# A state-space scan and an expert layer in one program: the opening's gates and logarithms taken from TensorE to VectorE and through DRAM

## The chip, the cores and the metric

The program runs on one core of one Trainium2 chip. The time is the device time of one execution in microseconds (us). Before the change it is 612.76 us, the median of 3 runs (612.08 to 614.41). One more execution was taken with the hardware profiler; it took 615.48 us, of which the span from the first to the last instruction is 613.8 us.

Engines are named as in the profile: PE is TensorE (PEld its weight loads), DVE is VectorE, ACT is ScalarE, POOL is GpSimd, SP is SyncE, which only issues DMAs here.

## The reference, cut to what matters

All numbers are float32. The first half is a chunked scan over 4 batches x 8 heads x 768 positions, the second half a layer of 4 experts on the 3072 tokens that come out of it.

```python
# per batch and head; chunks of 32 positions
log_a = log(clip(a, 1e-6, 1));  cum = cumsum(log_a in the chunk)
M     = (C @ B.T) * exp(cum[i] - cum[j]) * (i >= j)
y     = M @ x + (C @ state) * exp(cum)[:, None]
state = exp(cum[-1]) * state + sum_j exp(cum[-1] - cum[j]) * outer(B[j], x[j])
# tokens: y of all heads side by side, (3072, 256)
p   = domain_probs / (domain_probs.sum(-1) + 1e-9)
out = sum over experts e of  p[:, e] * (relu(y @ w1[e]) @ w2[e])
```

## The kernel before

The scan is worked off in 12 steps p of 64 positions (p = 2k + e: k is a chunk of 128 positions of each sequence, e its half), four sequences at a time. Each step needs: `scores` (C times B, L499), a decay matrix MT, `masked` (scores times MT, L675), `inner` products with x (L532), the product of C with the carried state (`cts` times S, L911, in `outputs`), and `state` (L541). For p under 3 the matrix MT comes from a running product on DVE (`scan`, L507) over rows of a that PE has spread over the partitions (`spread`, L652); from p = 3 on it is exponents on ACT (`decay`, L515) of sums of logarithms that come back from DRAM (`cum_d` as tiles `ab`) with a negated copy `neg` as bias. The carried state is faded by `dec`, the exponents of `ah`, which is read from another layout of the same sums in DRAM (`cumh_d`).

The expert layer multiplies with fewer products by sums of blocks: operand sums are made by POOL and DVE (`difference`, L1038), products are all one helper, L978 (`product`), results are gated (`gated`, L1013: Relu and gate in one DVE instruction, gate tiles read from `p_d` in DRAM), accumulated through ACT copies (L987, L992, L1278), and combined at the end (L1314). The last block's result is turned by PE (L1384), copied (L1397) and stored (L1389) piece by piece: piece 0 by two DMAs of POOL, the others by SP and ACT.

The order of the opening (L560 to L777) is written by hand: loads, clip of a, the scans of step 0, its scores, masks, inner products and state, and in between the work that prepares steps 1 and 2 and the later sums. In this part PE

- turns the gates `pc` (four transposes, L634), which ACT copies to `p_sb` (L636), and spreads the first gate over all partitions (`spread_gate`, L641, copied at L645); `p_sb` is stored to `p_d` late (L770);
- turns the logarithms (`turn_logs`, L688, copied at L689), sums them by products with a triangle `upto` (`sum_logs`, L693, copied at L696, stored at L699, L702 and L705), and makes the negated sums (`minus_logs`, L712, copied at L718);
- spreads the rows of part 1 of a (`spread(a_q, 1, ...)`) and of the next a (`a_q2`) before, between and behind the inner products.

Everything after that is given to a planner (`Plan`): each piece of work has engines that may do it, a cost, what it reads and writes, and a due time; PE's order is the given `line`, and the other engines' orders follow from a simulation of times that begins at constants (`now`, `START`, begin times for each engine). `OWN`, `SCORED`, `FILLED` and such say how many products stand ahead of which step and how banks of PSUM are handed out. Each engine then runs its own list strictly in order, and a DMA on SP, ACT or POOL stands in that engine's list as well. Eight semaphores serve SP's and ACT's DMAs in turn, so a DMA also waits until the one eight places ahead of it has landed.

The first products are four `plain_first` (two products each, on w1 blocks 0 to 3 and the first tokens yT0), then `scores(1)`, then `own_[:OWN]` products with w2, then `outputs(1)`.

Of the kernel before, what the change touches and what calls it, by code (L numbers as in the profile page):

```python
# [10 lines left out]
ALU = mybir.AluOpType  # L11
# [24 lines left out]
SCORED, OWN, LEAD, LEFT = 7, 4, 5, 4  # L36
FILLED, EARLY = 2, 4
# [33 lines left out]
class Plan:  # L71
# [109 lines left out]
    def run(self, line, at, begin):  # L181
# [17 lines left out]
        self.stall, self.port, self.bus = [], 0.0, begin["SP"] + 3  # L199
        self.lanes = [begin["SP"] + .5 * i for i in range(LANES)]  # L200
# [159 lines left out]
def kernel(  # L360
# [38 lines left out]
    p_d = tc.dram_tile([E * NC, 2, NSEQ, HALF], FP32, name="p_d")  # L399
    w_d = {}  # L400
# [8 lines left out]
    def some(n, shape, name, pool=const):  # L409
# [21 lines left out]
        "dram": [None, None],  # L431
# [26 lines left out]
    def load_carried(p, ah):  # L458
        k, e = divmod(p, 2)
        src = cumh_d.rearrange("(z k q) t e i -> k e z (q t) i", k=NC, q=NQ)[k, e]  # L460
        for z in range(NSEQ):
            nc.sync.dma_start(out=ah[:, z], in_=src[z].unsqueeze(1).to_broadcast([NH, N, HALF]))
# [11 lines left out]
    def load_w2(fb, w):  # L474
        e, f = divmod(fb, EPB)
        nc.sync.dma_start(
            out=w.rearrange("p (j m) -> p j m", j=JJ),
            in_=w2[e, f * FB:f * FB + FB].rearrange("(j p) m -> p j m", p=P))
# [84 lines left out]
    pc = const.tile([P, NSEQ, E, NC], FP32)  # L563
# [10 lines left out]

    for s, queue in enumerate((nc.sync, nc.scalar)):
        load_a(0, s, a_q, queue)
        load_heads(0, bct[0], slice(2 * s, 2 * s + 2), queue)
    nc.scalar.preload_act_table_set("natural_log_exp_and_others")
    for c in range(2):
        load_tokens(0, c, xt[0][:])  # L580
    nc.sync.dma_start(
        out=a_sb, in_=a.rearrange("c h s -> (c h) s").rearrange("(p r) s -> p r s", r=2))
    tmask = const.tile([P, NT], FP32)
    nc.vector.memset(tmask, 0.0)
    nc.vector.memset(a_q2, 0.0)
    for s in range(2):
        load_a(1, s, a_q2, nc.sync)
    for fb in range(4):
        load_w1(fb, homes["W"][fb])
    for fb in range(2):  # L590
        load_w2(fb, homes["W"][4 + fb])
# [18 lines left out]
    def ready(v, e):  # L610
# [11 lines left out]
    upto = const.tile([P, P], FP32)  # L622
    nc.gpsimd.memset(upto, 1.0)
    nc.gpsimd.affine_select(
        out=upto, in_=upto, compare_op=ALU.is_ge, fill=0.0, base=0, pattern=[[1, P]],
        channel_multiplier=-1)
    nc.gpsimd.memset(upto[:HALF, HALF:], 0.0)
    BANK = homes["bank"]
    rows = E * NC
    p_sb = homes["V"][0][:rows].rearrange("p e (z i) -> p e z i", z=NSEQ)  # L630

    def turn_gates(bank):
        for z in range(NSEQ):
            nc.tensor.transpose(  # L634
                bank[:rows, z * P:z * P + P], pc[:, z].rearrange("p e k -> p (e k)"), ident)
        nc.scalar.copy(  # L636
            out=p_sb.rearrange("p e z i -> p z e i"),
            in_=bank[:rows].rearrange("p (z e i) -> p z e i", z=NSEQ, e=2))

    def spread_gate(bank, gate):  # L640
        nc.tensor.matmul(  # L641
            out=bank[:, :FB], lhsT=ident[:rows, 0:1].to_broadcast([rows, P]),
            rhs=p_sb[:, 0].rearrange("p z i -> p (z i)"), start=True, stop=True,
            skip_group_check=True)
        nc.scalar.copy(  # L645
            out=gate[:, :2].rearrange("p c x -> p (c x)"), in_=bank[:, :FB])
# [36 lines left out]
    n = NSEQ * NC * NQ  # L683
    turned = homes["W"][-3][:, :2 * n].rearrange("p (t i) -> p t i", t=NT)

    def turn_logs(bank):
        for t in range(NT):
            nc.tensor.transpose(bank[:, FB + t * n:FB + t * n + n], a_sb[:, t], ident[:n, :n])  # L688
        nc.scalar.copy(out=turned, in_=bank[:, FB:FB + 2 * n].rearrange("p (t i) -> p t i", t=NT))  # L689

    def sum_logs(bank):
        for t in range(NT):
            nc.tensor.matmul(  # L693
                out=bank[:n, FB + t * P:FB + t * P + P], lhsT=turned[:, t], rhs=upto,
                start=True, stop=True, skip_group_check=True)
        nc.scalar.copy(  # L696
            out=homes["cum"][1].rearrange("p e (t i) -> p t e i", t=NT),
            in_=bank[:n, FB:].rearrange("p (t e i) -> p t e i", t=NT, e=2))
        nc.scalar.dma_start(  # L699
            out=cumh_d.rearrange("a t e i -> a e t i")[:, 1],  # L700
            in_=homes["cum"][1][:, 1].rearrange("p (t i) -> p t i", t=NT))
        nc.sync.dma_start(  # L702
            out=cum_d.rearrange("a e t i -> a (e t i)"),
            in_=homes["cum"][1].rearrange("p e x -> p (e x)"))
        nc.sync.dma_start(  # L705
            out=cumh_d.rearrange("a t e i -> a e t i")[:, 0],
            in_=homes["cum"][1][:, 0].rearrange("p (t i) -> p t i", t=NT))

    def minus_logs(bank):
        for s in range(2):  # L710
            for e in range(2):
                nc.tensor.matmul(  # L712
                    out=bank[HALF * s:HALF * s + HALF, FB + e * n:FB + e * n + n].rearrange(
                        "p (t i) -> p t i", t=NT),
                    lhsT=upto[:, HALF * e:HALF * e + HALF],
# [962 lines left out]
```

## Time and profile before

| what | value |
|---|---|
| median of 3 runs | 612.76 us (612.08 to 614.41) |
| profiled execution | 615.48 us, span 613.8 us, granted TensorE clock 0.997 |
| PE busy | 602.8 us, 98% of the span |
| DVE, ACT, POOL busy | 492.8, 276.3, 134.2 us |
| HBM | 72.79 MB read, 20.17 MB written |
| first product of the expert layer | 14.23 us after the span's start |
| last store issued | 609.19 us, end of the span 613.8 us |

How to read it: the busy share of PE says that the time is PE's work plus the few places where PE has none. Those places are the opening (before 14.23), single waits, and the end. The page's sections give shares over the whole span; a table by stage, the timeline and the chain of waits give the places. Times in the timeline and in the chain are us from the span's start. "issue" as a releaser means that the engine waited for nothing that the profile shows. A DMA's line shows the time that its issue took in the queue of the issuing engine, not the transfer.

### The profile page before, as it was taken

What the parts mean: (1) busy time and instruction counts of PE and PEld (TensorE: products, weight loads), DVE (VectorE), ACT (ScalarE), POOL (GpSimd) and SP (SyncE); (2) the same over time, 40 slices, a digit from 0 to 9 for tenths busy, and PEclk for the clock granted to TensorE, in tenths of its full rate; (3) what the DMA queues carried; (4) which work ended last, traced back from release to release, by engine and by line L of the source; (5) the groups of instructions that cost most, each with busy time, mean ns of one, the idle gap of its engine ahead of it and who ended that gap; (6) DMA issues with size and microseconds to landing.
All of it is one profiled execution on the core that took longest, in us unless ns stands there. A gap on an engine that the chain in (4) does not pass through costs nothing.

```text
span 613.8 us, 12211 instructions
## 1 busy us (share of the span) xinstructions
PE 602.8 (98%) x4528; PEld 517.5 (84%) x4528; DVE 492.8 (80%) x858; ACT 276.3 (45%) x623; POOL 134.2 (22%) x143
## 2 busy tenths in 40 slices
PE   9989999999999999999999999999999999999996
PEld 5768888888888888888888888878888888888886
DVE  5659999999999985687988988386785989575794
ACT  3338547675442626764343343434444242434440
POOL 4743554746500100358401000000000000000000
PEclk9989999999999999999999999999999999999999
DMA  6686578879723329763422425953241322954002
GB/s 179 169 250 208 170 191 257 252 230 285 254 77 115 89 33 336 223 224 131 144 82 72 125 34 161 303 170 114 69 133 67 110 72 45 362 190 131 1 0 53
DMA packets 98801, 93.78 MB, mean 153 GB/s; under 512 B 33405, under 2 KB 67933, under 8 KB 98741
## 3 DMA queue, kind: packets, MB, share of 16 engines
q1 hardware_dynamic: 97704, 92.10, 49.2%
q8 instruction: 36, 0.59, 0.4%
q10 hardware_dynamic: 940, 0.63, 0.4%
q0 software_dynamic: 96, 0.26, 0.2%
q14 instruction: 25, 0.20, 0.1%
HBM read 72.79 MB, written 20.17 MB: 151 GB/s over the span
## 4 chain that ended last, share of the span: by engine, by line
PE 89%; DVE 5%; issue 1%; DMA 1%; POOL 1%; ACT 1%; SPq 1%; POOLq 0%; DVEq 0%
PE bank L978 84%; PE bank L532 2%; DVE v L1013 1%; DVE v L1005 1%; PE bank L911 1%; DVE bank L1136 1%; PE bank L499 1%; PE bank L541 1%; POOL w L1038 1%; DMA gate<-p_d 1%; PE bank L652 0%; DMA xt<-in_xbc_dram 0%; DVE MT L520 0%; DVE MT L507 0%; DMA pr<-in_probs_dram 0%
## 5 line engine op out<-in xcount | busy, mean ns | idle before, releaser
L978 PE MATMUL bank<-v,w 128*128 128x256 f32 x1876 | 436.7, 381 | 4.1 <-issue 3.0
L978 PEld LDWEIGHTS bank<-v,w 128*128 128x128 f32 x1876 | 356.0, 191 | 55.5 <-issue 4.2
L978 PE MATMUL bank<-Y,w 128*128 128x256 f32 x692 | 177.2, 381 | 0.3 <-DVE bank L1136 0.3
L1005 DVE TENSOR_TENSOR v<-v,v 128x512 f32<-128x512 f32 x241 | 174.4, 744 | 1.8
L1278 ACT COPY v<-bank 128x512 f32<-128x512 f32 x120 | 70.4, 587 | 202.3 <-PE bank L978 198.3
L978 PEld LDWEIGHTS bank<-Y,w 128*128 128x128 f32 x692 | 130.5, 190 | 19.9 <-ACT v L987 0.9
L1013 DVE SCALAR_TENSOR_TENSOR v<-bank,gate 128x512 f32<-128x512 f32 x162 | 110.9, 686 | 43.5 <-PE bank L978 39.5
L1038 POOL TENSOR_TENSOR w<-w,w 128x512 f32<-128x512 f32 (+1 forms) x82 | 91.1, 1122 | 99.8 <-DMA xt<-in_xbc_dram 35.9
L992 ACT COPY bank<-v 128x512 f32<-128x512 f32 x141 | 81.6, 593 | 19.1 <-DVE v L1013 16.9
L987 ACT COPY v<-bank 128x512 f32<-128x512 f32 x111 | 65.2, 588 | 52.8 <-PE bank L978 45.9
L1136 DVE TENSOR_TENSOR bank<-bank,v 128x512 f32<-128x512 f32 x92 | 62.5, 693 | 32.4 <-PE bank L978 21.1
L1389 POOL DMA_DIRECT2D out_dram<-v x2 | 1.4, 713 | 261.6 <-DVE v L1397 261.6
L515 ACT ACTIVATE MT<-ab,neg 128x64 f32<-128x64 f32 x144 | 37.4, 339 | 0.0
L1005 DVE TENSOR_TENSOR v<-bank,v 128x512 f32<-128x512 f32 x30 | 20.6, 687 | 10.2 <-PE bank L978 7.4
L873 POOL TENSOR_TENSOR cts<-ctm,dec 128x512 f32<-128x512 f32 x11 | 14.9, 1356 | 47.4 <-DVE F L524 31.4
L1314 DVE TENSOR_TENSOR v<-v,v 128x256 f32<-128x256 f32 x64 | 24.2, 415 | 1.0 <-ACT v L1278 0.7
L1013 DVE SCALAR_TENSOR_TENSOR v<-v,gate 128x512 f32<-128x512 f32 x30 | 24.0, 798 | 0.5
L930 ACT COPY v<-bank 64x256 f32<-64x256 f32 (+1 forms) x33 | 12.3, 373 | 18.5 <-PE bank L541 15.4
L675 DVE TENSOR_TENSOR MT<-bank,MT 128x256 f32<-128x256 f32 x47 | 16.7, 412 | 0.7 <-PE bank L499 0.7
L520 DVE TENSOR_TENSOR MT<-MT,bound 128x512 f32<-128x512 f32 x18 | 15.6, 878 | 0.0
L489 ACT ACTIVATE ctm<-bct,tmask 128x256 f32<-128x256 f32 (+1 forms) x26 | 11.2, 485 | 9.4 <-POOL w L1038 5.1
L1005 POOL TENSOR_TENSOR v<-v,v 128x512 f32<-128x512 f32 x9 | 11.5, 1272 | 16.8 <-DVE v L1005 9.1
(96 smaller groups left out, 192.1 us busy)
## 6 DMA issues: line engine op xcount, KB each, us to landing
w<-w_d SPq DMA_DIRECT2D x128, 256.0 KB
w<-in_w_dram SPq DMA_DIRECT2D x72, 256.0 KB
w_d<-w SPq DMA_DIRECT2D x64, 256.0 KB
gate<-p_d SPq DMA_DIRECT2D x15, 384.0 KB
xt<-in_xbc_dram SPq DMA_DIRECT2D x48, 96.0 KB
ab<-cum_d SPq DMA_DIRECT2D x36, 128.0 KB
bct<-in_xbc_dram SPq DMA_DIRECT2D x5, 512.0 KB
out_dram<-v SPq DMA_DIRECT2D x144, 16.0 KB
```

The source lines that it names most:

```text
L515: nc.scalar.activation(out=MT[:, q, c, t], in_=ab[:, c, h], func=AF.Exp, bias=neg[:, e, t, i:i + 1])
L520: nc.vector.tensor_tensor(out=v, in0=v, in1=bound.unsqueeze(1).to_broadcast([P, 4 * n, HALF]), op=ALU.min)
L675: nc.vector.tensor_mul(v, bank[:, FB * half:FB * half + FB], v)
L978: nc.tensor.matmul(out=o, lhsT=w[:, j], rhs=x if half is None else x[:, j], start=(start and j == 0), stop=(j == 1), skip_group_check=True)
L987: act(.5, lambda e: nc.scalar.copy(out=flat(v), in_=bank.t), reads=[bank], writes=[v])
L992: act(.54 if to - lo > FB else .32, lambda e: nc.scalar.copy(out=bank.t[:, lo:to], in_=flat(v)[:, lo:to]), reads=[v], writes=[bank])
L1005: plan.add(engines, lambda e: (on(e).tensor_add if sign > 0 else on(e).tensor_sub)(flat(v), whole(x), whole(y)), reads=[x, y], writes=[v], ...
L1013: dve(D512, lambda e: nc.vector.scalar_tensor_tensor(out=h.t, in0=whole(x).rearrange("p (j m) -> p j m", j=JJ), scalar=0.0, in1=g.t[:, 2 * ...
L1038: (on(e).tensor_add if sign > 0 else on(e).tensor_sub)(out, x, y)
L1136: dve(D512, lambda e: (nc.vector.tensor_add if sign > 0 else nc.vector.tensor_sub)(to.t, bank.t, whole(x)), reads=[x, bank], writes=[to])
L1278: act(.5, lambda e: nc.scalar.copy(out=flat(v), in_=bank.t), reads=[bank], writes=[v], hold=HOLD)
L1314: plan.add(engines, lambda e: (on(e).tensor_add if sign > 0 else on(e).tensor_sub)(o[1](), x[1](), y[1]()), reads=[v for v in vs if v is n ...
```

## The change

In words: the gates `pc` are laid out in four padded groups of 32 columns, turned in 32 x 32 blocks by one DVE instruction, stored to `p_d` by four DMAs (two of SP, two of POOL), and the first gate tile is read back, spread over the partitions, by a DMA of SP. The logarithms are taken with a layout that puts each part's 64 positions side by side, and are summed by one DVE scan with a reset at each start; ACT's and SP's stores follow. The negated sums are made later, in the plan: a DVE turn, three stores to a new DRAM tensor `cumt_d`, two loads, and one ACT instruction (`minus_sums`; its DMAs stand on SP). All six late spreads stand ahead of the inner products; clip and memset of `a_q2` stand ahead of the first scans, and `a_q2` is loaded by ACT. Both halves of `bct` are loaded by SP. Three of the first four w1 blocks are loaded behind the gates' first two stores, the first two w2 blocks by POOL, one half of step 1's tokens (`xt[1]`) earlier, `ah` of step 1 by ACT. The first four gated results are made by Relu on ACT and a product on DVE (or POOL) instead of one DVE instruction. `upto` is gone; `bound` is made by itself. The last stores of piece 0 go by SP and ACT. Constants of the planner are changed; `OWN` goes from 4 to 5.

Program lists of the two kernels differ on PE in the opening (13 products and transposes fewer, one idle product more) and in the place of one product; from there on PE's order is the same. The lists of DVE, ACT, POOL and SP are ordered anew by the planner.

```diff
-SCORED, OWN, LEAD, LEFT = 7, 4, 5, 4
-FILLED, EARLY = 2, 4
+SCORED, OWN, LEAD, LEFT = 7, 5, 5, 4
+FILLED, EARLY = 3, 4
...
-    pc = const.tile([P, NSEQ, E, NC], FP32)
+    pc, turned = (homes["V"][0][:, i, :P] for i in range(2))
+    rows = E * NC
...
+    def store_gates(x, queue):
+        e, h = divmod(x, 2)
+        queue.dma_start(
+            out=p_d[:, e, :, 32 * h:32 * h + 32],
+            in_=turned[32 * x:32 * x + rows].rearrange("r (z i) -> r z i", z=NSEQ))
+
     for s, queue in enumerate((nc.sync, nc.scalar)):
         load_a(0, s, a_q, queue)
-        load_heads(0, bct[0], slice(2 * s, 2 * s + 2), queue)
+    for s in range(2):
+        load_heads(0, bct[0], slice(2 * s, 2 * s + 2))
     nc.scalar.preload_act_table_set("natural_log_exp_and_others")
+    tmask = const.tile([P, NT], FP32)
+    nc.vector.memset(tmask, 0.0)
+    nc.vector.memset(a_q2, 0.0)
+    for s in range(2):
+        load_a(1, s, a_q2, nc.scalar)
...
-    for s in range(2):
-        load_a(1, s, a_q2, nc.sync)
-    for fb in range(4):
-        load_w1(fb, homes["W"][fb])
-    for fb in range(2):
-        load_w2(fb, homes["W"][4 + fb])
+    load_w1(0, homes["W"][0])
...
+    def take_logs():
+        nc.scalar.activation(
+            out=logs.rearrange("p e (t i) -> p t e i", t=NT),
+            in_=a_sb.rearrange("p t (e i) -> p t e i", e=2), func=AF.Ln)
+
+    def sum_logs():
+        nc.vector.tensor_tensor_scan(
+            out=cum.rearrange("p e x -> p (e x)"), data0=reset[:ROWS].rearrange("p x i -> p (x i)"),
+            data1=logs.rearrange("p e x -> p (e x)"),
+            initial=0.0, op0=ALU.mult, op1=ALU.add)
+        for e, queue in ((1, nc.scalar), (0, nc.sync)):
+            queue.dma_start(
+                out=cumh_d.rearrange("a t e i -> a e t i")[:, e],
+                in_=cum[:, e].rearrange("p (t i) -> p t i", t=NT))
         nc.sync.dma_start(
+            out=cum_d.rearrange("a e t i -> a (e t i)"), in_=cum.rearrange("p e x -> p (e x)"))
+        load_tokens(1, 1, xt[1][:])
...
+    nc.vector.transpose(turned, pc)
+    for x in range(4):
+        store_gates(x, nc.gpsimd if x > 1 else nc.sync)
+    for fb in range(1, 4):
+        load_w1(fb, homes["W"][fb])
+    load_tokens(1, 0, xt[1][:])
+    nc.sync.dma_start(
+        out=homes["gate"][0][:, :2].rearrange("p c s -> p (c s)"),
+        in_=p_d[:1, 0].rearrange("x z i -> x (z i)").partition_broadcast(P))
+    ready(a_q2, 0)
...
-    turn_gates(four[2])
-    for s in range(2):
-        score(0, ctm[0], bct[0], seven, 0, s)
-    aside(2, seven[2])
-    spread(a_q, 1, four, 1, (3, 0))
+    score(0, ctm[0], bct[0], seven, 0, 0)
+    spread(a_q, 1, four, 1, ORDER[:2])
+    idle(four[2], 0, 1)
+    score(0, ctm[0], bct[0], seven, 0, 1)
+    spread(a_q, 1, four, 1, ORDER[2:])
+    spread(a_q2, 0, four, 0, ORDER)
...
+    fade_first(0)
+    aside(2, seven[2])
+    fade_first(1)
...
-    spread(a_q, 1, four, 1, (1, 2))
...
-    ready(a_q2, 0)
-    turn_logs(As[1])
     state(F[0], xt[0], As, 0, True)
-    spread(a_q2, 0, four, 0, ORDER)
-    sum_logs(As[0])
-    nc.sync.dma_start(out=p_d, in_=p_sb)
-    for c in range(2):
-        load_tokens(1, c, xt[1][:])
     keep_state(homes["A"][0], As, 0)
-    minus_logs(ys[0])
+    sum_logs()
+    for fb in range(2):
+        load_w2(fb, homes["W"][4 + fb], nc.gpsimd)
...
-    now, START = 9.4, 11.3
+    now, START = 9.7, 10.3
...
+        by, queue = ("SP", nc.sync) if p > 1 else ("ACT", nc.scalar)
+        plan.add({by: ISSUE * 4}, lambda e: load_carried(p, s["ah"].t, queue), lag=LANDING + 256 / 190, kb=256,
+                 pieces=4, part=[s["ah"]], reads=[cd])
...
+    def gated_aside(x, g, n):
+        h = value("V")
+        act(.5, lambda e: nc.scalar.activation(out=flat(h), in_=x.t, func=AF.Relu), reads=[x], writes=[h])
+        plan.add(B512, lambda e: on(e).tensor_mul(
+            h.t, h.t, g.t[:, 2 * n:2 * n + 2].rearrange("p c s -> p (c s)").unsqueeze(1).to_broadcast(
+                [P, JJ, FB])), reads=[g], writes=[h], two=True)
+        return h
...
-        return seq, gated(b, gate_of(0, fb), 0)
+        return seq, gated_aside(b, gate_of(0, fb), 0)
...
-            by = ((nc.sync, "SP"), (nc.scalar, "ACT")) if n else ((nc.gpsimd, "POOL"),) * 2
+            by = ((nc.sync, "SP"), (nc.scalar, "ACT"))
...
+    def minus_sums():
+        v, d = value("V"), value("dram")
+        dve(.4, lambda e: nc.vector.transpose(v.t[:ROWS, 0], sums.t.rearrange("p e x -> p (e x)")),
+            reads=[sums], writes=[v])
...
+        act(.35, lambda e: nc.scalar.mul(neg.t, neg.t, -1.0), writes=[neg])
```

## The prediction

> **What bounds the kernel now.** I read the page's busy times first, then its clock and queue rows, then a table by stage, the timeline of PE around its one hole, and the chain of waits in the opening.
>
> The page; then the table by stage (stretch, its length, busy us and instructions by engine, granted clock, DMA share, GB/s):
>
> ```profile
> PE 602.8 (98%) x4528; PEld 517.5 (84%) x4528; DVE 492.8 (80%) x858; ACT 276.3 (45%) x623; POOL 134.2 (22%) x143
> ...
> PEclk9989999999999999999999999999999999999999
> ...
> q8 instruction: 36, 0.59, 0.4%
> ```
>
> ```profile
> 9.40:14.23 4.83, 4.65 (x136) 3.15 (x135) 2.24 (x7) 1.85 (x5) 2.74 (x7) 1.00 0.82 252
> 14.23:25.96 11.73, 11.45 (x82) 9.40 (x80) 9.83 (x20) 2.44 (x8) 9.17 (x12) 1.00 0.56 165
> 25.96:37.10 11.14, 11.14 (x317) 8.71 (x318) 5.52 (x15) 6.21 (x17) 7.19 (x8) 1.00 0.79 227
> 37.10:40.11 3.01, 0.00 (x1) 0.00 (x0) 3.01 (x6) 0.31 (x2) 1.98 (x3) 1.00 0.79 270
> 40.11:44.20 4.09, 4.09 (x12) 3.30 (x12) 1.85 (x4) 0.37 (x1) 0.56 (x1) 0.58 0.72 220
> 44.20:100.00 55.80, 55.45 (x549) 46.24 (x548) 52.97 (x88) 34.68 (x99) 25.71 (x23) 1.00 0.66 196
> 100.00:600.00 500.00, 499.01 (x3317) 434.87 (x3316) 406.72 (x688) 225.78 (x483) 80.82 (x70) 1.00 0.48 146
> ```
>
> PE is the bound: from 44.2 to 600 it is idle for 1.3 us. The change touches none of those products (FILLED, for the planner's banks, moves by one), so it can act in four places: before the first product at 14.23, in the wait at 25.96, in the hole at 37.10 with the slow clock behind it (0.58), and behind the last product. The timeline shows the wait and the hole, the chain what the opening's end is made of (start, length, what):
>
> ```profile
> 25.96 0.67 PE L911 MATMUL bank<-cts,S 32*32 32x128 f32 x32 [0.29 <-POOL cts L873]
> ...
> 40.11 4.22 PE L978 MATMUL bank<-v,w 128*128 128x256 f32 x11 [3.01 <-issue]
> ```
>
> ```profile
> 5.44 1.86 DVE MT L507 x3
> ...
> 9.47 1.35 PE bank L532 x64
> 10.82 0.59 PE bank L652 x8
> 11.41 0.33 PE bank L688 x2
> ...
> 12.13 0.45 PE bank L541 x30
> 12.59 0.62 PE bank L652 x16
> 13.20 0.62 PE bank L693 x4
> 13.82 0.02 issue
> ```
>
> **The opening.** From the first scan (5.44) to the first product (14.23) the old path is 2.43 (four scans) + 1.53 (second scores, masks; until 9.40) + 1.42 (inner products) + 0.59 (spreads) + 0.33 (logarithms turned) + 0.39 (ACT's copy of them) + 0.45 (state) + 0.62 (spreads) + 0.62 (sums) + 0.41 (negated sums) = 8.79. Turn, copy, sums and negated sums go: 1.75. The gates' turn (0.60) and spread (0.69) lay in PE's waits; they give nothing. The six late spreads move ahead of the inner products. There the last two of part 1 (0.30) and a_q2's four (0.65) stand behind the last scan, because they overwrite banks that scans read; they cover the masks (0.42) and most of the old 1.53, whose other cause, the second half of bct (masked until 7.70), is issued earlier, by SP at once behind the first. New path: 2.43 + 0.95 + 1.42 + 0.55 (state; yT's copies, 0.42, lie beside it) = 5.35, so 3.44 less.
>
> Against it: a_q2's clip (0.42) and memset (0.06) now stand ahead of the scans on DVE. All four scans are queued behind them, and PE, POOL's ends and ACT's aside wait for the scans. a_q2 moves from SP to ACT, behind the table load (1.28 us in the trace). If ACT's queue issues it beside that load, from 2.8 on in 2 x 0.58, and it lands 1.0 later (ACT's first half of a: issue ended at 2.75, DVE's clip began at 3.76), it is there at 5.0, and with the gates' turn and the clip the scans start at 5.7. If it is issued behind the load, it is there at 6.3 and the scans start at 6.8; with the 1.5 that SP's a_q2 took to land, 7.3. I take 6.3, the middle, 0.86 late. VectorE's turn of the gates (128x128; the 128x512 form takes 0.69, so 0.2 to 0.4) fits ahead of it. Opening: 3.44 - 0.86 = **2.6**, first product at 11.65 (11.0 to 12.7).
>
> Who comes too late then? The first w1 no longer waits behind a_q2 on SP and lands before its old 9.8; the other three, behind two gate stores (0.56 each), are due 1.7 us apart: hidden. The first gate goes SP store at about 6.7, load at 10.4, landed near 13; DVE asks for it after the sum scan (0.6) and four scans, at 14.7: hidden by 1.7, beyond that each us holds three scans, F, S and the masks on DVE. SP waits at the sums' stores with xt's second half, two w2 and bct behind it, as it did until 14.24. POOL issues two gate stores ahead of its end copies (0.82 and 0.60 in the last rows) and two w2: 2.9 us; the w2 are due 7.8 us after the first product. ACT issues four loads of ah (2.5) with three of four new Relu copies (0.59 each) behind them: the carried chain ends some 9 us after the first product, PE asks at 12.5, against 11.7 before, so the 0.29 goes: **-0.3**. The negated sums go through DRAM with 5 DMAs behind eight of ab; ACT wants them at 50.7 (first exponents): hidden by several us, else ACT's snaps wait and PE with them. DVE's total hardly moves: four gate products from SBUF (0.74 for 0.69), one scan, two transposes, two F fewer. Reordering by new planner constants may open waits of the kind seen (0.2 to 0.7 each): 0 to 2, **+0.6**.
>
> **The hole.** "issue" means that no semaphore held PE, in the middle of a product. q8 carried 36 packets of 16 KB of instructions (0.59 MB), and PE has 2 x 4,528: 252 for each packet. So I read q8 as PE's instruction feed, and the hole as PE having run out. The trace's packets on q8 start at 12.2, 15.8, 28.2, then 37.55, inside the hole, after SP had issued some 2.5 MB from 25 to 32; PE resumed at 40.11. The change takes 20 matmuls and 20 loads from PE ahead of it (4 + 2 + 2 + 4 + 8) and adds 2 + 2: 36 instructions fewer, so PE reaches 18 products further on what it holds, 18 x 0.224 = 4.0 us, past the 3.01. If the packet comes when the DMA backlog clears, the hole goes, and with it the slow clock, 4.09 x (1 - 0.58) = 1.7: **-4.7**. If it comes a fixed time after PE's place, about 2.6 later here, 1.6 us stay. Worst, it is as long: 0. I take -4.7, since SP's loads of that stretch are spread wider (one waits for a gate buffer, bct behind a POOL sum).
>
> [...]
>
> **The end.** POOL's stores of the first piece (0.82, 0.60 from 608.11) go to SP and ACT, about 0.5 each; ACT's stands ahead of a copy of 0.27. The last stores, issued at 609.19, are not moved: -0.7 to +0.3, **-0.2**.
>
> **Sum.** -2.6 - 0.3 - 4.7 - 0.2 + 0.6 = -7.2: the profiled execution's 615.48 (span 613.8 and 1.7 around it) becomes 608.3. It stands 2.7 above the median 612.76. If that is constant, 605.6; if timed runs have a shorter hole, the hole can give only 2.0 there, and 608.3 stays. Nothing separates these; I take the middle, **607.0**, own range 604.5 to 609.
>
> **Rivals.** *The hole stays* (moved by 18 products): 612.76 - 2.6 - 0.3 - 0.2 + 0.6 = 610.3, to 611.5 with more waits. For it: the packet may be late because PE's sequencer asks late, at a place in the code; then the 36 instructions shift the hole and its length stays, and one late packet can't tell. Against: the other packets came in time with DMA less loaded, and 4.0 is more than 3.01. 0.2.
>
> *The clock falls in the opening.* Between 6.4 and 9.7 PE now waits scan by scan, about half idle; a granted 0.58 over the inner and first products costs 1.7 as after the hole, and a_q2 late 1.0 more: 608.7 to 609.7. Against: 4.29 to 9.40 ran at 1.00 with PE busy for 4.83 of 5.11, and an idle matmul is put in. 0.12. [...]
>
> *The gates come late, and it is slower.* The nearest round trip through DRAM, the sums' (stored 14.24, dec at 22.48), took 8.2; from 6.7 that is 14.9, where DVE asks. DVE's list from the first gate product to the last mask is 7.3 us in the trace's rows, to 22.0; PE asks for the masks at 24.1, so 2.1 are free, and past 17 each us costs PE one. Slower by over 0.5% needs all gains and 3.1 more eaten: landing past 25. Against: only two small stores and one load. 0.07.
>
> Nothing comes of the opening and the hole is absent in timed runs: about 612.5, 0.06.
>
> **Chances.** Forecast 0.55. 0.5%, about what can be told from no change here, is 3.1 us: faster means below 609.7: the forecast, a third of the first rival, most of the second: 0.67. Within: 0.24; slower: 0.09. Range 604.5 to 611.5: forecast's low end, first rival's high end.
>
> **What would show it.** First L965 product at 11.0 to 12.7, the first scan near 6.3; no "issue" of over 1 us on PE, and a 9 in the third place of PEclk, now 8; outputs at L898 waiting for nothing; PE idle under 3 us from 44 to 600. Wrong: a hole with a clock near 0.58 anywhere, or DVE L1011 ended by a DMA of gate.

## The result and the profile after

The changed kernel takes 611.81 us in the median of 20 runs (609.60 to 614.07), the kernel before, on the same chip, 613.85 (20 runs, 612.08 to 616.05). The ratio is 0.9962 with a 95% interval of 0.9948 to 0.9975: faster by 0.4%, where 0.9% was forecast (607.0 from 612.76). That is within the 0.5% that the prediction counted as no change, and 0.3 us outside its range. The profiled execution took 612.63 us, its span is 610.91 (before 613.77).

The page of the changed kernel:

```profile
PE 601.5 (98%) x4510; PEld 516.8 (85%) x4510; DVE 494.8 (81%) x855; ACT 277.9 (45%) x623; POOL 143.8 (24%) x152
...
PEclk7999999999999999999999999999999999999999
...
q8 instruction: 35, 0.57, 0.4%
```

The low digit of the clock has moved from the third place to the first. The table by stage (columns as in the prediction):

```profile
8.46:14.97 6.51, 6.38 (x141) 4.87 (x139) 2.39 (x7) 1.24 (x4) 4.68 (x11) 0.50 0.82 257
14.97:27.33 12.36, 12.36 (x84) 10.29 (x84) 11.42 (x22) 4.33 (x11) 6.25 (x9) 0.99 0.55 154
27.33:39.18 11.85, 11.00 (x317) 8.27 (x316) 8.24 (x17) 6.60 (x19) 7.55 (x9) 1.00 0.67 205
44.20:100.00 55.80, 54.80 (x547) 45.87 (x546) 53.44 (x88) 35.89 (x105) 30.93 (x27) 1.00 0.78 225
100.00:600.00 500.00, 498.75 (x3317) 434.96 (x3316) 405.31 (x680) 223.75 (x475) 87.70 (x77) 1.00 0.47 145
```

In the last 6.5 us of the opening the granted clock is 0.50, and there is no stretch with PE at 0.00 any more. PE's idle time from 44 to 100 is 1.0 us; it was 0.35. PE's timeline where the wait, the hole and the slow clock stood:

```profile
27.33 0.67 PE L898 MATMUL bank<-cts,S 32*32 32x128 f32 x32
...
33.56 1.99 PE L965 MATMUL bank<-v,w 128*128 128x256 f32 x8 [0.84 <-DVE MT L661]
...
39.68 1.99 PE L965 MATMUL bank<-v,w 128*128 128x256 f32 x8 [0.50 <-DVE v L1000]
```

The outputs (L898) wait for nothing, and no product waits for "issue"; small waits for DVE stand there instead. The chain of waits in the opening (start, length, what):

```profile
3.11 3.07 DMA v<-in_a_dram
...
6.61 0.69 DVE MT L508
...
8.57 0.72 PE bank L664 x2
...
10.36 1.69 PE bank L638 x19
12.05 2.00 PE bank L533 x58
```

The scans start at 6.61, held by a_q2 (the DMA of `v`, landed at 6.2). The spreads (L638) and inner products (L533, 2.00; it was 1.35) run at the granted 0.50: a spread takes 629 to 684 ns from 9.28 on, 374 to 424 at 7.35 to 8.20, a score 416 to 472, 267 to 318 at 5.95. Rows as long as these at 0.50 are called half speed below, whatever the granted clock reads. The first product stands at 14.97 instead of the forecast 11.65.

The span's difference of -2.86 us, by three places that both traces show: the first product comes 0.74 later (14.23, 14.97); from there to PE's last matmul it is 2.65 shorter (594.60, 591.95: the hole of 3.01 and the slow clock of 1.7 are gone, PE's single waits together grew from 1.62 to 3.60); from the last matmul to the end it is 0.95 shorter (4.94, 3.99).

### The profile page after: what moved, and what is told of

It reads as the page before. It is cut to its first block, busy times and chain, and to the rows that moved or that the text cites. A ratio compares the mean times of both kernels' runs of the same rounds, so it can differ in the third digit from the quotient of the medians.

```text
span 610.9 us, 12231 instructions
## 1 busy us (share of the span) xinstructions
PE 601.5 (98%) x4510; PEld 516.8 (85%) x4510; DVE 494.8 (81%) x855; ACT 277.9 (45%) x623; POOL 143.8 (24%) x152
## 4 chain that ended last, share of the span: by engine, by line
PE 91%; DVE 4%; DMA 3%; issue 1%; SPq 1%; POOL 0%; ACT 0%; DVEq 0%; ACTq 0%; POOLq 0%
PE bank L965 86%; PE bank L533 2%; DMA bct<-in_xbc_dram 1%; DVE v L1000 1%; DMA xt<-in_xbc_dram 1%; PE bank L898 1%; PE bank L500 1%; PE bank L638 1%; DMA v<-in_a_dram 1%; PE bank L542 0%; SPq L443 0%; DVE MT L521 0%; DVE bank L1132 0%; DVE Y L1104 0%; DVE MT L661 0%
## 5 line engine op out<-in xcount | busy, mean ns | idle before, releaser
L1000 DVE SCALAR_TENSOR_TENSOR v<-bank,gate 128x512 f32<-128x512 f32 x158 | 108.4, 686 | 42.7 <-PE bank L965 38.4
L1034 POOL TENSOR_TENSOR w<-w,w 128x512 f32<-128x512 f32 (+1 forms) x82 | 95.3, 1174 | 89.7 <-DMA xt<-in_xbc_dram 31.2
L979 ACT COPY bank<-v 128x512 f32<-128x512 f32 x141 | 81.6, 593 | 21.6 <-DVE v L1000 15.7
L1310 DVE TENSOR_TENSOR v<-v,v 128x256 f32<-128x256 f32 x59 | 22.6, 419 | 0.9 <-ACT v L1274 0.7
L1000 DVE SCALAR_TENSOR_TENSOR v<-v,gate 128x512 f32<-128x512 f32 x30 | 22.3, 742 | 0.4
L521 DVE TENSOR_TENSOR MT<-MT,bound 128x512 f32<-128x512 f32 x18 | 16.6, 933 | 1.5 <-ACT MT L516 1.5
L1310 POOL TENSOR_TENSOR v<-v,v 128x256 f32<-128x256 f32 x8 | 6.3, 789 | 29.9 <-DVE v L992 17.0
```

The source lines that it names most:

```text
L521: nc.vector.tensor_tensor(out=v, in0=v, in1=bound.unsqueeze(1).to_broadcast([P, 4 * n, HALF]), op=ALU.min)
L979: act(.54 if to - lo > FB else .32, lambda e: nc.scalar.copy(out=bank.t[:, lo:to], in_=flat(v)[:, lo:to]), reads=[v], writes=[bank])
L1000: dve(D512, lambda e: nc.vector.scalar_tensor_tensor(out=h.t, in0=whole(x).rearrange("p (j m) -> p j m", j=JJ), scalar=0.0, in1=g.t[:, 2 * ...
L1034: (on(e).tensor_add if sign > 0 else on(e).tensor_sub)(out, x, y)
L1310: plan.add(engines, lambda e: (on(e).tensor_add if sign > 0 else on(e).tensor_sub)(o[1](), x[1](), y[1]()), reads=[v for v in vs if v is n ...
```

## The experiments

Ratios are to the kernel before on the same chip, with 95% intervals.

**e1_warm, e14_warm_again: is it the clock?** Both are the changed kernel with

```diff
+    for i in range(2):
+        idle(BANK[7], 3, 4)
-    spread(a_q, 1, four, 1, ORDER[:2])
+    spread(a_q, 1, four, 1, ORDER[:1])
+    idle(BANK[7], 3, 4)
+    spread(a_q, 1, four, 1, ORDER[1:2])
```

> The changed kernel with three more idle products of 128x128 in the opening: two behind the first half of step 0's scores (PE is idle there for 0.74 us) and one between the first two spreads that wait for scans. Theory 'clock': in the changed kernel's profiled execution PE's half idle stretch from 6.6 to 9.2 lets the clock fall to 0.5 from 8.46 to 15.29; with PE filled it stays at 1.00, the inner products take 1.4 again (2.07), the spreads of part 1 and of a_q2 1.5 (2.8), the first product stands at 12.5 to 13.2 instead of 14.97, and the profiled execution becomes 610.3 to 611.0 (612.63). Timed runs: those with a low clock go, so the median falls by about 1 us, 0.998 of the changed kernel, 0.994 of the kernel before. Rival 'late a_q2': the time goes to the late landing of a_q2 alone and the clock costs nothing that the end sees: first product within 0.5 of 14.97, no change of the time.

> e1 once more: the changed kernel with three more idle products between 6.6 and 9.2. In e1 six executions lay between 610.5 and 611.7. Theory 'half speed in the opening': again 610.4 to 611.2 in the median, 0.6 to 1.2 below the changed kernel's 611.7 to 611.8, and a narrow spread. If e1's six were luck: median 611.5 or more.

e1: 610.77 us (610.48 to 611.72), ratio 0.9947 (0.9930 to 0.9964); first product 13.32, inner products 1.25, profiled execution 610.61. e14: 610.83 (610.04 to 615.44), ratio 0.9942 (0.9922 to 0.9963). The median is 1.0 below the changed kernel's, twice, but the two were not run against each other on one chip, and the intervals of the ratios overlap with the changed kernel's. Part of an execution lies outside the span: at most 1.8 us in all 104 executions of the kernel before whose span is on record, but 2.0 or more in 25 of 49 executions of the kernels with these three idle products (e1, e3, e14, e15, e16). No trace shows what it is; it takes a part of what e1 wins in its span (median 608.6 against 609.9).

e14's profiled execution is the one of 615.44: PE ran at half speed until 17.1 there, idle products and all, and the first product came at 18.06, while the granted clock of that profile reads 1.00 throughout. So the idle products do not exclude a slow opening.

**e2_clip_late, e3_warm_late: is it a_q2?** e2 is the changed kernel with `ready(a_q2, 0)` moved from ahead of the first scans to behind the four of step 0; e3 is e2 with e1's edit.

> The changed kernel with clip and memset of a_q2 on VectorE moved behind the four scans of step 0 (ACT still loads it at the same place). Theory 'late a_q2': the scans start at 5.3 to 5.5 instead of 6.61, all that follows comes 1.0 to 1.2 earlier, and the half idle stretch of PE is shorter; if the clock stays up as well, the first product comes at about 11.7 and the profiled execution at 609.5; if the clock still falls, at 13.9 and 611.5. Rival 'the second half of bct decides' (its masks by ACT begin at 6.84): the scores of the second sequence half come no earlier than 7.6, the first masks at 8.7 at the earliest, and the first product at 12 to 12.6 with the clock up.

> Both edits together: three more idle products and the clip of a_q2 behind the scans. If clock and a_q2 are the two causes of the late first product, the first product stands at 11.6 to 12.3 and the profiled execution at 608.5 to 609.7, 0.991 of the kernel before; if the new waits behind the opening grow as PE comes to them earlier (an operand of VectorE that is made at a fixed time), half or more of that is lost there: 610.5 to 611.5.

e2: scans from 5.29, ACT's second pair of masks from 6.26 (6.84 in the changed kernel), first product at **11.28**. The profiled execution is the fastest, 610.09 us: of the 3.7 us that it leads the changed kernel's profile by at the first product, 2.5 are left at the end. The median is 611.97 us (610.09 to 612.20), ratio 0.9959 (0.9944 to 0.9974). Seven of the nine executions have a mean clock of 0.996 or 0.997 and took 611.65 to 612.20; the two others have 0.999 and 1.000 and took 610.09 and 610.41. One stretch like that in the profile of before, behind the hole (0.50 from 40.14 to 43.55, 3.4 us), would give such a mean and such a difference; where it lay, no profile of them shows.

e3: first product 12.56, 610.86, ratio 0.9951 (0.9933 to 0.9969). The three idle products put its first product 1.3 behind e2's.

In e1, e2 and e3 the first product stands at 13.32, 11.28 and 12.56, and the spans are 608.24, 608.38 and 608.29: an earlier opening no longer makes an earlier end. Where e2's lead went is in its lists of PE, DVE and ACT:

```profile
21.43 4.58 PE L965 MATMUL bank<-v,w 128*128 128x256 f32 x20 [2.38 <-DVE MT L508]
```

```profile
20.09 0.69 DVE L1011 TENSOR_TENSOR v<-v,gate 128x512 f32<-128x512 f32 x1 [1.84 <-ACT v L1010]
20.69 0.68 DVE L508 TENSOR_TENSOR_SCAN MT<-bank,identr 128x256 f32<-128x256 f32 x1
```

```profile
16.84 2.56 ACTq L463 DMA_DIRECT2D ah<-cumh_d  x4
19.45 1.57 ACT L1010 ACTIVATE v<-bank 128x512 f32<-128x512 f32 x3 [5.53 <-DMA ah<-cumh_d]
```

Read upwards: ACT issues the four loads of ah, which read what the sums' stores write (issued from 11.80), only at 16.84; three Relus stand behind them; a gate product of DVE waits for the second Relu, the fourth scan of step 2 stands behind that, and the first w2 product needs the bank that this scan reads. However early the opening ends, this product starts at 21.4 to 21.8 (e1, e2, e3). The wait is the changed kernel's own when its opening runs at full speed from 8.0 or 8.6 on: 1.88 at 22.39 in e13, 1.02 at 21.72 in e11, both for the same scan.

**e5_one_gate, e15_warm_ah_sp: the two ways out of ACT's queue.** e5 is e2 with the gates in one DVE instruction again; e15 is e3 with the loads of ah on SP again.

```diff
-        return seq, gated_aside(b, gate_of(0, fb), 0)
+        return seq, gated(b, gate_of(0, fb), 0)      # e5
-        by, queue = ("SP", nc.sync) if p > 1 else ("ACT", nc.scalar)
+        by, queue = "SP", nc.sync                    # e15
```

> e2 with one edit more: the first four results are gated again by one VectorE instruction from PSUM, without ACT's Relu copies (the planner orders the other engines' lists anew). In e2 PE waits 2.38 us at 21.43 for a scan's bank, the scan stands behind a gate product on DVE, that behind a Relu of ACT, and three Relus behind four loads of ah that ACT issues only when the sums' store has landed (16.8 to 19.4). Theory 'ACT's queue': without Relus that wait is gone and the first w2 product comes at 19.0 to 19.5. Then two cases. 'The carried chain is the next floor': cts is finished at 26 as in e2 (26.24), PE waits for it at L898 for 2 to 2.7 us, and the span stays at 608.4 plus or minus 0.4. 'Nothing else was late': outputs at 23.7 to 24.2 without a wait, the span is 2.0 to 2.4 shorter, 606.2. Rival 'the scans are late by themselves': the wait of about 2 us for MT L508 stays.

> e3 (idle products, clip of a_q2 late) with the loads of ah for step 1 on SP again, the Relu copies of the gates as in the changed kernel. Theory 'ACT's queue': without the four loads ahead of them the Relus come as PE finishes, the wait of 1.07 us at 21.4 is gone, and the outputs of step 1 start 1 us earlier than in e3 (25.91), unless the carried chain, now issued by SP behind its other loads, comes later: then a wait for cts of 0.5 to 2 us at L898. Rival 'DVE's scans are late by themselves': the wait at the first w2 product stays at 1 us.

Both take the wait away: the first w2 product at 20.00 and 20.34, outputs of step 1 at 24.51 and 24.85 (26.29 in e2, 25.91 in e3), without a wait for cts. The carried chain was not the next floor. But neither is faster by its ratio: e5 610.93 (609.34 to 613.33), 0.9956 (0.9938 to 0.9973), as e2; e15 612.84 (612.02 to 618.27), 0.9988 (0.9969 to 1.0008), slower than e3. Up to 73.69 e5's lead goes in one place:

```profile
73.69 1.90 PE L965 MATMUL bank<-v,w 128*128 128x256 f32 x6 [2.04 <-DVE bank L1132]
```

The same product starts at 73.69 in e2 too, after a wait of 0.60. Behind the longer wait e5's profile has a granted clock of 0.50 from 74.78 to 78.19, half of 3.4 us lost, and its span is 1.3 longer than e2's. Six of e5's twelve executions have a mean clock of 0.997 or less and a median of 611.8, the six others one of 610.3. In e15 a wait of 1.73 at 57.01 takes the lead, for DVE L996.

**e6_own7, e16_warm_one6: more products ahead of the outputs.** e5 with `OWN` 7; e3 with e5's gates and `OWN` 6.

> e5 with OWN at 7 instead of 5: eight more product passes of w2 (1.8 us) ahead of the outputs of step 1, taken from those behind. If the carried chain is the floor (cts at 26), PE now reaches the outputs at 25.6, the wait for cts shrinks by 1.8 against e5 and the span with it, to 606.3 to 607, if nothing behind comes later by that; PE's work itself is the same. If another operand (w2 of the third and fourth block, loaded late) sets the place, a wait of 1 to 2 us at a w2 product stands there instead and nothing is won.

> e3 with the first four gates in one VectorE instruction (e5's edit) and OWN at 6: an attempt at a better version. No wait at the first w2 product, outputs of step 1 at 26.5 to 27 without a wait, those of step 2 at 33.0; then, if the loads behind the sums come at times of their own (ah, ab from SP at 60 to 73), the gain over e3 is eaten by waits at 45 and 74 and the median is 610.5 to 611; if not, 609.5.

e6: 611.39, 0.9965 (0.9948 to 0.9982); e16: 612.91, 0.9979 (0.9962 to 0.9996). The premise of e6 (a wait for cts in e5) was wrong; its waits are others, 4.6 us between 18 and 106. In e16 1.83 us at 74.2 again.

**e12_less_dve: is DVE the floor at 74?** e5 with the decay matrices' bound (L521) on 4 of 64 columns.

> e5 with less work on VectorE: the instruction that bounds the decay matrices (L521, 128x512, 0.68 us, two for each step from p = 3) does 4 of 64 columns, so the decay matrices are not bounded above the diagonal. The order of all engines is that of e5. In e5 PE stood 1.5 us earlier than in e2 at the outputs of step 1 and 2.0 earlier at those of step 2, and lost all of it at 45.6 (0.70) and 73.7 (2.04, for DVE L1132), where DVE is 7.3 to 8.0 us busy of 8. Theory 'DVE's full list is the floor between 44 and 80': both waits fall under 0.4, the outputs of step 3 come at 78 to 79 (81.62 in e5, 79.9 in e2), the span is 606 to 607.3. Rival 'the loads behind the sums (ah, ab) come at times of their own': the waits stay, outputs of step 3 later than 80, span 608.5 or more.

Inconclusive for its main question. 609.93 (608.80 to 611.61), 0.9942 (0.9920 to 0.9965), the lowest median of all, but this kernel leaves out a part of the work. In the profile cts came late (a wait of 1.49 at 26.72), so PE reached the product of 73.69 only at 73.5, and still waited until 74.39. DVE was busy for 7.72 of the 8 us from 66 to 74 all the same (8.00 in e5). Whether DVE's work or one of the loads behind the sums is the floor there, stays open.

**e4_before_again, e7_before_36, e8_before_last, e10_before_72, e11_after_36: the hole and the end.** e4 is the kernel before again. e7, e10 (before) and e11 (changed) get 9, 18 and 9 tiny idle products, 4 instructions each, ahead of the first spreads:

```diff
+    for i in range(9):
+        nc.tensor.matmul(out=BANK[7][:32, :1], lhsT=one.to_broadcast([P, 32]), rhs=one, ...)
     spread(a_q, 0, four, 0, ORDER)
```

e8 is the kernel before with the last stores of piece 0 by SP and ACT:

```diff
-            by = ((nc.sync, "SP"), (nc.scalar, "ACT")) if n else ((nc.gpsimd, "POOL"),) * 2
+            by = ((nc.sync, "SP"), (nc.scalar, "ACT"))
```

> The kernel before once more, for a second profile of it. If the hole of 3.01 us at 37.10 belongs to the program (a packet of instructions that comes late behind the loads of that stretch), it is there again at the same product with 2 to 4 us, and the clock is low behind it; if it was an accident of that one execution, it is not there, and the span is 3 to 5 us shorter than 613.8.

> The kernel before with nine tiny idle products (32x1 outputs, 36 instructions of PE) put ahead of the first spreads, where PE waits for the load of a. In its two profiles PE stops at the same product, at 37.10 for 3.01 us and at 37.34 for 2.48, and starts again 2.3 to 2.5 after the fourth packet on q8 (37.55, 37.48). Theory 'PE has run out of instructions': it now stops 18 matmul records earlier (the last products and part of the state, about 1.5 to 2 us earlier, near 35.5), and if the packet comes at the same time (37.5) the hole grows to 4 to 4.7 us. 'The feed answers to PE's place': it stops earlier and the hole keeps 2.5 to 3.0. 'It belongs to that product': the same product, the same length.

> The kernel before with eighteen tiny idle products (72 instructions of PE) ahead of the first spreads; e7, with nine, stopped at 35.09 for 1.29 us instead of 37.1 to 37.3 for 2.5 to 3.0, no slow clock behind it, and started again 2.34 after the fourth packet of q8. Theory 'the feed answers to PE's place': PE stops earlier again (33 to 34.5, in the outputs or products before them), the fourth packet comes earlier too (32 to 33.5), and the hole is at most 1.3 us or gone; the time is that of the good executions of before or 0.5 to 1.5 less, 611 to 612.5. Theory 'PE runs out, the packet comes at a time of its own': packet at 34 or later, the hole 3 us and longer, 613 to 615.

> The changed kernel with nine tiny idle products (36 instructions of PE) ahead of the first spreads, where PE waits: as many instructions as the change takes from PE ahead of the hole. If those 36 were what removed the hole (the prediction's step), it comes back: 1 to 3 us of 'issue' between 35 and 40, and the time rises by as much, to 613 to 614. If the hole is gone because the packets come earlier in the changed kernel (fourth packet at 33 to 37 with fewer instructions used up), it stays away, and the time is that of e9 within 0.5.

> The kernel before with one edit: the last stores of piece 0 by SP and ACT instead of POOL. From PE's last matmul to the end of the span it was 4.94 and 5.29 in two profiles of before, and 3.95 to 3.99 in the changed kernel and in e1 to e3. If the store by POOL is the cause, 4.0 here, a gain of 1.0 to 1.3 of the span instead of the 0.2 of the prediction; ratio about 0.998. If the end's gain comes of something else (less traffic at the end), 4.9 to 5.3 as before and no change.

PE's timeline, in the order e4, e8, e7, e10, e11, e16 (one line of each):

```profile
39.82 2.76 PE L978 MATMUL bank<-v,w 128*128 128x256 f32 x9 [2.48 <-issue]
```

```profile
39.66 2.53 PE L978 MATMUL bank<-v,w 128*128 128x256 f32 x11 [2.04 <-issue]
```

```profile
36.38 0.34 PE L541 MATMUL bank<-xt,F 64*32 64x64 f32 x13 [1.29 <-issue]
```

```profile
38.91 0.46 PE L541 MATMUL bank<-xt,F 64*32 64x64 f32 x31 [0.87 <-issue]
```

```profile
36.98 3.33 PE L969 MATMUL bank<-v,w 128*128 128x256 f32 x13 [0.85 <-issue]
```

```profile
33.28 0.45 PE L902 MATMUL bank<-cts,S 32*32 32x128 f32 x15 [0.87 <-issue]
```

The same stops, counted in matmul records (PE's matmul instructions in the trace, each with one weight load) from the start of the trace and against the last packet on q8:

| kernel | records before the stop | stop | length | restart after the packet |
|---|---|---|---|---|
| before | 601 | 37.10 | 3.01 | 2.56 |
| e4 | 601 | 37.34 | 2.48 | 2.34 |
| e8 | 601 | 37.62 | 2.04 | 2.53 |
| e7, 18 records more | 601 | 35.09 | 1.29 | 2.34 |
| e10, 36 records more | 601 | 38.04 | 0.87 | 2.38 |
| e11, 18 records more than after | 599 | 36.13 | 0.85 | 2.34 |
| e16 | 473 | 32.41 | 0.87 | 2.55 |

The program's place differs (a product, a state, an output), the count does not: 601, give or take missing records, or 128 records less, 256 instructions at two for each record. By the pages a packet on q8 comes to 252 of PE's instructions in before (36 packets for 2 x 4,528) and 258 in the changed kernel (35 for 2 x 4,510), so 128 records are about one packet. And PE goes on 2.3 to 2.6 us after a packet in all seven. So "issue" is read here as PE out of instructions, and q8 as its feed. What the counts also show is that the packet has no time of its own: it came at 37.55 in before, at 34.04 in e7 and at 34.64 in e11, and in e7 and e10 the hole became shorter, not longer, with more instructions ahead of it.

The packet follows PE's place. In all eighteen profiles the fourth packet starts 0.0 to 3.7 us after PE's 473rd record, 128 ahead of the 601st. In the six profiles that stop at the 601st or 599th, PE had worked off these records before the packet had come and 2.3 to 2.6 us had passed. In the kernel before they take 3.0 us, and the packet comes 3.5 after the 473rd; in the changed kernel they take 7.3 (0.5 of it a wait), because 18 more of the long products stand among them, and the packet comes 1.1 after. In e11 they take 2.6 again, the packet comes 1.1 after the 473rd, and the hole is 0.85. What makes the packet come after 0.0 or after 3.7 us stays open.

In times: e11 611.66 (610.44 to 613.14), 0.9965 (0.9946 to 0.9984), no different from the changed kernel (0.9962), though the hole of 0.85 is back. e10 615.98, 1.0019 (0.9996 to 1.0042): a wait of 1.0 at 13.0 and a granted clock of 0.50 behind it put the first product at 16.55, so its time says nothing of the hole. e7 was run once, 612.54.

e8: 613.00 (611.62 to 615.43), 0.9991 (0.9973 to 1.0008), too small for the ratio, but the trace shows it: 4.1 us from the last matmul to the end. The four profiles with POOL's stores (before, e4, e7, e10) have 4.9 to 5.4, the changed kernel and all its variants 3.9 to 4.5. With POOL's stores the span ended 4.1 us after the last issue was done (4.4 in e4), with SP's and ACT's 2.7 in e8 and 2.6 in the changed kernel (3.1 in e6 and e16).

**e9_after_again.** The changed kernel a second time.

> The changed kernel once more, for a second profile and for times beside e10 to e12 on one chip. By theory 'clock' its executions are of two kinds: with the clock down in the opening (mean 0.993, first product near 15, 612.2) and with the clock up (0.999 to 1.0, first product at 13.0 to 13.4, 610.4). If a profile with the clock up comes, its scans start at 6.5 all the same (a_q2's clip), and PE waits 0.5 to 1.0 for a scan's bank near 21.5, since the Relus behind the loads of ah are as late as in e1.

611.74 (610.50 to 613.37), 0.9964 (0.9944 to 0.9984). Its profile has a clock of 1.00 in every row, and the first product nevertheless at 15.26. The groups of PE from 5.9 to 13, for the changed kernel, e9 and e2 (instructions, then busy us and mean ns of one):

```profile
L638 PE MATMUL bank<-v,own 32*64 32x256 f32 x32 | 4.0, 578 | 0.7 <-DVE MT L508 0.7
```

```profile
L638 PE MATMUL bank<-v,own 32*64 32x256 f32 x32 | 4.5, 643 | 0.0
L500 PE MATMUL bank<-ctm,bct 32*64 32x128 f32 x32 | 2.3, 430 | 0.0
```

```profile
L638 PE MATMUL bank<-v,own 32*64 32x256 f32 x32 | 2.3, 383 | 0.0
L500 PE MATMUL bank<-ctm,bct 32*64 32x128 f32 x32 | 1.3, 280 | 0.0
```

The same spread takes 383 ns or 643, the same score 280 or 430. In e9 PE's rows had until 13.7 the length that those of the changed kernel have at a granted 0.50 (spreads 629 to 684 ns, scores 416 to 472), while the granted clock of e9 reads 1.00. In every profile the first spreads or the idle products ahead of them have the long form; it ends between 4.2 and 6.8 in most, at 8.0 in e13, 8.6 in e11, 13.7 in e9, 17.1 in e14.

These are two different things. In the changed kernel's profile PE was at full speed from 5.2 (spreads of 424 ns at 7.35) and fell back at 8.46, behind a wait of 0.74, and the granted clock shows it (0.50 from 8.46 to 15.29). In e9 and e14 PE had not come up at all, and the granted clock does not show that.

**e13_no_idle.** The changed kernel without `idle(BANK[6], 0, 4)` and `idle(BANK[7], 0, 3)`.

> The changed kernel without the first two idle products (128x512 and 128x384), so that PE does nothing before 4.1. In all traces PE's first rows take the length of a half clock (spreads 655 ns, 374 to 424 later), though the granted clock reads 1.00 there, and the rows change to full length at 4.2 to 6.2 in most executions, 8.6 and 13.8 in two. Theory 'the slow opening is PE at half speed': without the early idle products PE is at half speed until 9 or later, the first product comes at 15 or later, and the median is 612.0 to 613, 0.3 to 1.2 above the changed kernel. Rival 'the opening does not reach the end': first product later, median as the changed kernel's (611.8) within 0.3.

The expectation was wrong: 611.10 (610.18 to 611.67), 0.9950 (0.9931 to 0.9969), first product at 12.74, full speed from 8.0. PE comes up without the early idle products too.

What the recorded falls of the clock did to the times can be counted. A mean clock of 0.994 or less, as 6.8 us at 0.50 give it in the changed kernel's profile, came in 12 of 32 executions of the changed kernel (after and e9); their median is 612.2, that of the other 20 is 610.8. It came in none of 25 of e1, e3 and e14, which fill PE's half idle stretch. That the filling does it is not shown: it came in none of 18 of e11 and e13 either, which fill nothing there, and e11's median is that of the changed kernel all the same, with its hole of 0.85 and a wait of 1.02 at 21.72.

## Why the prediction was wrong

Step by step, as it was put:

- **The opening, -2.6 (first product at 11.65): failed, +0.74.** The list of what goes was nearly right: in e2 and e5, with PE at full speed and a_q2's clip out of the way, the first product came at 11.28 and 11.49 (10.8 by the prediction's path without a_q2). Two terms were not. The sum put nothing for the clock: PE's half speed was left to the second rival, with 0.12, and it is what happened in the profile. With a_q2 as it is and full speed from 8.0 or 8.6, the first product came at 12.74 and 12.93 (e13, e11), so that half speed cost 2.0 to 2.2 of the 14.97. And a_q2, put at 0.86, cost 1.3 to 1.6 (12.74 and 12.93 against 11.28 and 11.49): it landed at 6.2 and the scans began at 6.61, inside the range given (5.7 to 7.3) but late of its middle. A fall of the clock is on record in 12 of 32 executions; how many more had a PE that came up late, as in e9, the record can't tell. The argument against the rival ("4.29 to 9.40 ran at 1.00 with PE busy") rested on the granted clock, which reads 1.00 where the rows are at half speed (spreads of 655 ns at 4.29, then 374 to 424). e9 and e14 stayed slow until 13.7 and 17.1 with no stop of PE over 0.3 us from 0.85 on. What brings PE to full speed, no run shows.
- **The new waits, +0.6: mis-sized.** All single waits together grew by 2.0 in the profile (1.62 to 3.60) where +0.6 and -0.3 were forecast, and by 3.1 in e2 (to 4.76). Behind an opening at full speed the largest is the 2.38 at 21.43 (e2; 1.88 in e13). The prediction named it: "ACT issues four loads of ah (2.5) with three of four new Relu copies (0.59 each) behind them", and then priced only the loads' own consumer, the carried chain, not the Relus' consumers (gate, scan, bank, product). This is the step to learn from: a queue with waiting DMA issues was listed, and the prediction did not ask who needs what stands behind them.
- **The wait for cts, -0.3: right** in the profile (L898 waits for nothing), not always: 0.85 in e9, 0.87 in e14.
- **The hole, -4.7: right in the profiles, too large for the median.** It is gone in both profiles of the changed kernel, by the count that the prediction gave: 18 records fewer ahead of the 601st, so that PE gets there at 43.0, 6.2 after the packet. e11 put the 18 back, and the hole came back. The condition on which the prediction chose this case, "if the packet comes when the DMA backlog clears", fell: the packet's time moves with PE. So the choice was right by luck: by its other case, a packet at a fixed time behind PE's place, it had 1.6 us staying. The size was that of one profile. Of 104 executions of the kernel before with a recorded clock, 55 have a mean clock of 0.998 and more and a median of 613.1, 49 a lower one and 615.0; the profiled 615.48 belongs to the second kind. The prediction saw that the profile stood 2.7 above the median and took half of it off; a slow stretch like the one behind the hole (1.7) is in fewer than half of the executions.
- **The end, -0.2: mis-sized, -0.95.** The store's own issue was priced, not how long after it the span ends.
- **The gates through DRAM:** no wait in the changed kernel, as forecast. In e2 and e5, with an earlier opening, DVE does wait for the first gate (1.70 and 1.39, until 15.8 and 15.7): the rival's place was right, its price was not reached.

The sum by the profile: 3.3 missing in the opening, 1.7 in the waits, 0.75 more at the end, so -2.9 for -7.2. Of the rivals, "the clock falls in the opening" happened; its 608.7 to 609.7 left out the waits behind. Of the prediction's signs all came but one: no "issue" over 1 us, a 9 in the third place of PEclk, outputs that wait for nothing and PE idle for 2.3 us from 44 to 600. The first product alone was not where it should be.

What e1, e2, e3, e5 and e15 show together is that mending the opening alone would not have given the forecast: a wait at 21.4, then one at 57 or 74, takes the lead back. Among the kernels that do the whole work e1 has the lowest ratios (0.9947 and 0.9942; the changed kernel 0.9962 and 0.9964), with e13 and e3 beside it (0.9950, 0.9951); the intervals overlap.

## What to carry to other kernels

When a DMA issue moves to another engine's queue, follow the list of that engine past the moved instruction: who needs the next results, and when, if the issue waits for its semaphore. Work taken out of a start-up gives its time only if nothing behind it is tied to other times; look for the next wait before summing. Judge TensorE's speed by the length of equal rows, not by the granted clock alone (a spread took 643 ns in e9 and 383 in e2, both at a clock of 1.00), and a stop with "issue" by the count of instructions since the start (six of the seven stops here at the 601st or 599th record). And before a profile is set against a median, see whether its execution is of the kind that makes the median (e2's was not).

## What the runs showed of the hardware

- PE stopped at the 601st matmul record (once at the 473rd) in seven profiles, for 0.85 to 3.01 us, and went on 2.34 to 2.56 after a packet on q8. The two places are 128 records of two instructions each apart, 256; a packet on q8 has 16 KB in the traces of before and of the changed kernel and comes to 252 and 258 of PE's instructions there. In before the stop stands behind 317 records in 11.14 us with a DMA share of 0.79.
- PE at half speed with a granted clock of 1.00: spreads of 643 ns in e9 (383 in e2; 629 to 684 at a granted 0.50 in the changed kernel), up to 13.7 us into the program in e9 and 17.1 in e14. What ends it was not found.
- The granted clock fell to 0.50 inside the program in five of eighteen profiles, each time 0.0 to 1.3 us after the end of a stop of PE: behind 3.01 us in before, 2.48 in e4, 2.04 in e5, 1.00 in e10 and 0.74 in the changed kernel, for 3.4 us (6.8 in the changed kernel). Stops of 1.7 to 2.4 us in e2, e8, e13, e15 and e16 had no such fall behind them.
- A span that ends with stores issued by POOL ended 4.1 and 4.4 us after the last issue (before, e4), with stores by SP and ACT 2.6 to 3.1 (changed kernel, e6, e8, e16).
